# Halves of an attention head added by VectorE, one head split by GpSimd, a new order, and identity products among the first scores

## The chip, the cores and the metric

The kernel runs on one core of one Trainium2 chip. The metric is device time in microseconds (us) of one execution; the kernel before takes 1424.79 us, the median of 3 runs (1421.05 to 1426.22).

## The reference

Three blocks in a row, all in fp32:

```python
# attention: B=4, H=8, S=1152, D=64; 32 heads
q_pool = q.reshape(B, H, 576, 2, 64).mean(axis=3)
scores = q_pool @ k.T / 8;  attn = softmax(scores);  o = attn @ v        # 576 x 1152 per head
# mixer on x = (4, 576, 512)
h = relu(x.T @ w_tok1) @ w_tok2;  u = x + h.T;  x = u + relu(u @ w_ch1) @ w_ch2
# Fourier mixing, normalisation, channel block
u = x + real(fft2(x));  out = u + relu(norm(u) @ w1) @ w2
```

## The kernel before, in words

All fp32 products are made of fp32r parts: a number is split into a high part (ScalarE copies it with rounding) and a low part (the difference, by VectorE or GpSimd), and TensorE adds high·high, high·low and low·high.

`Plan` holds every operation of the program with an engine, a cost, a due time and the buffers that it takes. `order` issues, on each engine, the ready operation with the earliest due time; the table `SHIFT` adds a number to the due time of each kind of operation, so that table sets the order of the whole program. Each engine then works through its own list in order.

**The heads.** There are 32 heads (`g`), each with two units of 256 and 320 query columns (`UNITS`). The first eight (`g < ALONE`) run without a mixer beside them. For them `first_peaks` makes scores of 116 query rows by 384 keys (L684, 15 pairs of products a head), VectorE takes the maximum of each (L690), the maxima are turned by TensorE (L716) and laid into the query tile (L721), and `first_unit` makes the scores again, turned (L753), takes the exponential (L758) and multiplies by the values (L764). These values have a 65th column of ones, so the sum of each row comes out as a 65th row.

For the other 24 heads `peaks` makes the scores (L650) into one tile `m` of three banks, VectorE takes the maximum (L657), ScalarE the exponential and its sum (L660); `unit` turns it by TensorE (L803), ScalarE and VectorE split it (L807, L810), and the products with the values (L817) gather in one bank, `av`, of which there is one. The stationary side there holds the high parts of the values in columns 0 to 63 and the low parts in 64 to 127, so that the result has two halves, in partitions 0 to 63 and 64 to 127, that must still be added. ScalarE copies all 128 partitions into the tile `xtr` (L824).

**Turning the head.** `head_out` brings `xtr` back to rows of queries, in five blocks of 128 columns. For `g < ALONE` these are five transposes of 65 rows (L846). For the others they are five fp32 products with `twice`, two identities of 64 on top of each other (L848), which turn the tile and add its halves at once; an fp32 product stands in the trace as two. VectorE then scales the result (L860).

**The start.** `first_pair` loads the queries and keys of heads 0 and 1 and splits them for itself: sum of the two query halves (L560), high part (L562), low part (L564), and for the keys a high part (L572), a low part (L574) and a second copy (L576), the sums and the low parts on VectorE. Pairs of later heads are split by GpSimd (L600 to L610). `warm` puts 14 products of the identity, 512 columns each, in front of the scores (L586). Weights come as float64 and are made fp32 by ScalarE, GpSimd and VectorE all through the attention (L373 to L395).

Of the kernel before, what the change touches and what calls it, by code (L numbers as in the profile page):

```python
# [10 lines left out]
F32 = mybir.dt.float32  # L11
# [12 lines left out]
HQ = NQ // 2  # L24
# [20 lines left out]
ALONE = 8  # L45
NPH = 5
# [16 lines left out]
    "fourth": -81.45, "cvld": 14.04, "cabs": 225.41, "cclamp": 629.43, "cshift": 1065.51, "csign": 830.73,  # L63
    "cexp": 67.76, "cword": 44.09, "cmul": 212.45, "cadd": 527.83, "chi": 417.69, "csub": -302.75, "cvst":
    166.15, "cs": -293.69, "warm.": 694.45, "l.": -703.76, "q.": -145.41, "qh.": 219.14, "ql.": -134.29, "kh.":
    609.88, "kl.": -314.67, "M.": -448.03, "mr.": -385.51, "zh.": 237.47, "mr2.": -990.19, "zl.": -889.77,
    "mT.": 127.71, "mrow.": -636.35, "vld": -251.06, "S.": -1317.58, "exp.": 564.5, "AV.": 48.91, "xe.": 343.25,
# [7 lines left out]
    "sqrt": -1015.85, "fcld": -48.8, "fchi": -168.21, "fclo": 1157.76, "nyld": -154.7, "nyh": -411.21, "fld":  # L75
    152.94, "FPUT": 83.63, "DFT": -196.52, "Zh": 512.01, "Zl": -101.21, "PB": -31.29, "PA": -31.21, "bs": 8.24,
# [157 lines left out]
def tile_attention_moe_fnet(  # L234
# [43 lines left out]
    eps = base.tile([128, 1], F32, name="eps")  # L278
    rooted = base.tile([128, 1], F32, name="rooted")
    own = base.tile([128, len(QE)], F32, name="own")  # L280
    twice = base.tile([128, D], F32, name="twice")

# [1422 lines left out]
```

## Time and profile before

| | us |
|---|---|
| median of 3 runs (lowest, highest) | 1424.79 (1421.05, 1426.22) |
| the profiled execution, its own time | 1423.28 |
| its span in the trace | 1421.5 |
| TensorE matmuls busy in the span | 1388.5 |
| VectorE, ScalarE, GpSimd busy | 964.2, 770.1, 573.0 |

The span is what the trace covers; 1.8 us of the profiled execution's time lie around it. Busy times are unions, and a matmul's end is modelled, so that two matmuls one behind the other overlap in the trace.

### The profile page before, as it was taken

Reading aid. Unit: us, or ns where it says so; the run is one execution under the profiler, and the core shown is the slowest. Engines: PE = TensorE matmul, PEld = TensorE weight load, DVE = VectorE, ACT = ScalarE, POOL = GpSimd, SP = SyncE. Lnnn points to the kernel's source line nnn. Section 1 sums busy time; section 2 is a strip of 40 time slices with the busy share of each in tenths; the row PEclk is TensorE's granted clock in tenths of the full one; section 3 lists DMA queues with packets and bytes.
Section 4 is the critical chain, followed back from the end, with each engine's and each line's share of the span. In section 5 each row is a group of like instructions: output and inputs, shape, how many; then the busy total and the mean of one; then the engine's idle time right before and its main releaser. Section 6 shows DMA issues by size and latency. Waiting matters only on the chain.

```text
span 1421.5 us, 24599 instructions
## 1 busy us (share of the span) xinstructions
PE 1388.5 (98%) x9139; PEld 1284.5 (90%) x9139; DVE 964.2 (68%) x1782; ACT 770.1 (54%) x1534; POOL 573.0 (40%) x473
## 2 busy tenths in 40 slices
PE   7999999999999999999999999999999999999998
PEld 6777779999998999999999999999899888888887
DVE  7667568778886788777678884677757357656442
ACT  4554567666767667667666764322335245344330
POOL 4766776646765556677374561011110000000000
PEclk8999999999999999999999999999999999999999
DMA  6778777666678667776686545875274554543532
GB/s 184 209 200 223 196 221 232 205 188 211 205 204 249 191 191 215 207 215 207 197 239 192 160 149 171 259 234 158 78 237 124 208 183 167 196 156 137 204 115 93
DMA packets 112177, 270.36 MB, mean 190 GB/s; under 512 B 9971, under 2 KB 37748, under 8 KB 111767
## 3 DMA queue, kind: packets, MB, share of 16 engines
q1 hardware_dynamic: 112058, 268.79, 61.8%
q8 instruction: 72, 1.18, 0.3%
q14 instruction: 47, 0.39, 0.1%
HBM read 191.15 MB, written 44.86 MB: 166 GB/s over the span
## 4 chain that ended last, share of the span: by engine, by line
PE 87%; DMA 4%; DVE 3%; ACT 3%; issue 1%; SPq 1%; POOL 0%; ACTq 0%; DVEq 0%; POOLq 0%
PE bank L1449 9%; PE bank L1006 9%; PE m L650 8%; PE bank L986 8%; PE av L817 7%; PE y L1508 7%; PE bank L803 5%; PE c L1508 5%; PE av L764 3%; PE bank L684 2%; PE tr L986 2%; PE bank L1319 2%; PE y L1341 2%; PE s L753 2%; DMA slot<-in_wm_dram 2%; PE tr L803 2%
## 5 line engine op out<-in xcount | busy, mean ns | idle before, releaser
L657 DVE TENSOR_REDUCE nm<-m 128x1 f32<-128x1152 f32 (+1 forms) x120 | 162.3, 1352 | 36.6 <-PE m L650 33.5
L807 ACT ACTIVATE ph<-bank 128x320 fp32r<-128x320 f32 (+2 forms) x253 | 116.3, 477 | 100.7 <-PE bank L803 95.0
L660 ACT ACTIVATE s<-m,nm 128x1152 f32<-128x1152 f32 (+1 forms) x120 | 146.5, 1221 | 30.6 <-DVE nm L657 30.2
L1449 PE MATMUL bank<-tt,wc 128*128 128x320 f32 x1008 | 158.2, 311 | 4.6 <-DVE e L1463 4.6
L1449 PEld LDWEIGHTS bank<-tt,wc 128*128 128x128 f32 x1008 | 149.9, 188 | 12.8 <-DVE e L1463 10.6
L650 PE MATMUL m<-kk,qq 128*128 128x384 f32 (+1 forms) x720 | 151.0, 344 | 4.3 <-ACT s L660 4.2
L810 DVE TENSOR_TENSOR pl<-bank,ph 128x320 fp32r<-128x320 f32 (+2 forms) x253 | 130.7, 532 | 30.4 <-ACT ph L807 28.9
L1006 PE MATMUL bank<-h,w 128*128 128x256 f32 (+1 forms) x954 | 150.1, 300 | 0.0
L375 POOL TENSOR_SCALAR slot<-slot 128x512 f32<-128x512 f32 (+2 forms) x62 | 118.5, 1912 | 58.0 <-ACT slot L373 54.6
L986 PE MATMUL bank<-ut,w 128*128 128x256 f32 (+1 forms) x900 | 138.0, 297 | 0.0
L388 POOL TENSOR_TENSOR slot<-slot 128x512 f32<-128x512 f32 (+2 forms) x62 | 81.7, 1317 | 131.8 <-DVE slot L383 118.2
L1006 PEld LDWEIGHTS bank<-h,w 128*128 128x128 f32 x954 | 133.2, 189 | 0.3 <-DVE yt L1015 0.2
L817 PE MATMUL av<-ph,vv 128*128 128x256 f32 (+1 forms) x432 | 132.8, 324 | 0.0
L650 PEld LDWEIGHTS m<-kk,qq 128*128 128x128 f32 (+1 forms) x720 | 118.3, 179 | 11.3 <-ACT s L660 6.3
L986 PEld LDWEIGHTS bank<-ut,w 128*128 128x128 f32 x900 | 125.1, 189 | 0.0
L817 PE MATMUL av<-pl,vv 128*128 128x256 f32 (+1 forms) x432 | 120.2, 295 | 0.0
L803 PE MATMUL bank<-ident,s 128*128 128x128 f32 (+1 forms) x809 | 116.0, 262 | 2.6 <-DVE pl L810 2.4
L1463 DVE TENSOR_TENSOR e<-bank,e 128x320 f32<-128x320 f32 x96 | 47.2, 491 | 99.2 <-PE bank L1449 54.2
L1508 PE MATMUL y<-v,hp 128*128 128x512 f32 x432 | 104.2, 391 | 0.0
L803 PEld LDWEIGHTS bank<-ident,s 128*128 128x128 f32 (+1 forms) x809 | 96.7, 141 | 7.0 <-DVE pl L810 3.5
L1508 PEld LDWEIGHTS y<-v,hp 128*128 128x128 f32 x432 | 80.4, 188 | 16.4
L1015 DVE TENSOR_TENSOR yt<-bank,yt 128x320 f32<-128x320 f32 (+1 forms) x159 | 72.1, 455 | 28.7 <-PE bank L1006 26.7
(190 smaller groups left out, 2929.8 us busy)
## 6 DMA issues: line engine op xcount, KB each, us to landing
w<-wb_d SPq DMA_DIRECT2D x96, 512.0 KB, 4.9
slot<-in_wm_dram SPq DMA_DIRECT2D x56, 512.0 KB, 5.6
v<-w_d SPq DMA_DIRECT2D x24, 1024.0 KB, 5.5
raw<-w_d SPq DMA_DIRECT2D x24, 896.0 KB, 6.7
kk<-kx SPq DMA_DIRECT2D x66, 288.0 KB, 3.3
wb_d<-slot SPq DMA_DIRECT2D x24, 512.0 KB, 6.1
v<-in_v_dram SPq DMA_DIRECT2D x32, 292.5 KB, 3.9
qx<-in_qT_dram SPq DMA_DIRECT2D x15, 576.0 KB, 5.4
```

Source lines behind the costliest of these rows:

```text
L375: a = add("cclamp", "P", 0.155 + n * 0.00347, due, lambda: nc.gpsimd.tensor_scalar(out=f32(hi()), in0=f32(hi()), scalar1=F64_LO, scalar2=F ...
L650: nc.tensor.matmul(m.t[:n, :KW], qq.t[:r, t, q0:q0 + n], kk.t[:r, c * KW:(c + 1) * KW], start=(t == 0), stop=(t == 1))
L657: a = add("mx" + own_place, "V", t_dve(S), d + 0.05, lambda n=n, j=j: nc.vector.tensor_reduce(out=nm.t[:n, j:j + 1], in_=m_tile[0][:n, :, ...
L660: o = add("exp" + own_place, "A", t_act(S) + 0.18, d + 0.1, lambda s=s, n=n, j=j: nc.scalar.activation(out=s.t[:n].rearrange("p (c n) -> p ...
L803: nc.tensor.transpose(ps.t[:, at:at + r], made[j][0].t[:r, c * 128:(c + 1) * 128], ident[:r, :r])
L807: a = add("hi", "A", t_act(n), due + 0.1, lambda ps=ps, ph=ph, n=n: nc.scalar.activation(out=ph.t[:, :n], in_=ps.t[:, :n], func=AF.Copy), ...
L810: b = add("lo", "V", t_dve(n), due + 0.2, lambda ps=ps, ph=ph, pl=pl, n=n: nc.vector.tensor_tensor(out=pl.t[:, :n], in0=ps.t[:, :n], in1=f ...
L817: nc.tensor.matmul(po.t[:, :nq], vv.t[:, c].rearrange("p s d -> p (s d)"), x.t[:, k * nq:(k + 1) * nq], start=c == 0 and x is ph, stop=c = ...
L986: mms.append(lambda ps, k=len(mms), kk=kk, wi=wi, xi=xi, t0=t0, n=n: nc.tensor.matmul(ps[:, :n], view("p (s k n) -> p s k n", s=2, k=4)[:, ...
L1006: mms.append(lambda ps, k=len(mms), x=x, wi=wi, hi=hi, cc=cc, t0=t0, n=n: nc.tensor.matmul(ps[:, :n], ww[x][2]("p (s n) -> p s n", s=2)[:, ...
L1449: nc.tensor.matmul(ps.t[:, :PH], w.t[:, wi, k, 128 * kk:128 * kk + 128], x.t[:, xi, kk], start=(first and m == 0), stop=(last and m == 5), ...
L1508: nc.tensor.matmul(y.t, h.t[:, k, hi, j * 128:(j + 1) * 128], v.t[:, wi, k], start=(q == 0 and k == 0 and n == 0), stop=(q == 7 and k == 1 ...
```

## The change

It does five things.

- The 24 later heads are turned by five transposes of 65 rows, as the first eight are. `twice` is gone, and `xtr` has 65 partitions.
- So the halves are added before: ScalarE copies the upper 64 partitions of `av` (L836 of the changed file), and a new VectorE operation, `xa`, adds the lower 64 from `av` (L838), twice a head. `av` is held until that has run.
- Head 1's sum of query halves and the low parts of its keys (one operation of 576 columns, three of 384) go from VectorE to GpSimd.
- The warm-up has 22 products of 256 columns in place of 14 of 512, and 28 more such products stand among the score products of heads 0 and 1 (table `BETWEEN`).
- `SHIFT` has new numbers, so that every engine's list is in a new order.

```diff
+BETWEEN = ((0, 0, 0, 1, 0, 0, 13, 0, 0, 0, 0, 4, 1, 1, 0),
+           (8,) + (0,) * 14)
-    "fourth": -81.45, "cvld": 14.04, "cabs": 225.41, "cclamp": 629.43, "cshift": 1065.51, "csign": 830.73,
+    "fourth": -186.94, "cvld": 20.26, "cabs": 361.34, "cclamp": 955.96, "cshift": 1159.55, "csign": 719.06,
...
-            t = sp.tile([128, 640], F32, name=f"xtr{i}", bufs=1)
+            t = sp.tile([65, 640], F32, name=f"xtr{i}", bufs=1)
...
+                side = nc.gpsimd if g else nc.vector
...
-                    o = add("q.", "V", t_dve(b - a), d, lambda q=q: nc.vector.tensor_tensor(
+                    o = add(*(("q.", "V", t_dve(b - a)) if g == 0 else ("qp.", "P", t_pool(b - a))), d, lambda q=q, side=side: side.tensor_tensor(
...
-                    l = add("kl.", "V", t_dve(b - a), d, lambda k=k, kk=kk, a=a, b=b: nc.vector.tensor_tensor(
+                    l = add(*(("kl.", "V", t_dve(b - a)) if g == 0 else ("kp.", "P", t_pool(b - a))), d, lambda k=k, kk=kk, a=a, b=b, side=side: side.tensor_tensor(
...
-                for _ in range(WARM):
-                    nc.tensor.matmul(bank.t.rearrange("p (k n) -> p k n", k=4), ident_r,
-                                     ident_r[:, None, :].to_broadcast([128, 4, 128]), start=True, stop=True)
+                for _ in range(WARM * 8 // 5):
+                    idle_product()
...
+        spare = Buf(av_r)
+
+        def idle_product():
+            nc.tensor.matmul(spare.t[:, :256].rearrange("p (k n) -> p k n", k=2), ident_r,
+                             ident_r[:, None, :].to_broadcast([128, 2, 128]), start=True, stop=True)
...
+                    idle = BETWEEN[g][n_tops] if g < 2 else 0
+
-                    def scores(bank=bank, q0=QE[j], c=c):
+                    def scores(bank=bank, q0=QE[j], c=c, idle=idle):
+                        for _ in range(idle):
+                            idle_product()
...
-            return add("xe" + own_place, "A", t_act(nq), i + 1.7, lambda: nc.scalar.activation(
-                out=x.t[:, q0:q0 + nq], in_=po.t[:, :nq], func=AF.Copy), [o], new=[] if half else [x], uses=[po] + [x] * half)
+            def dst():
+                return x.t[:64, q0:q0 + nq]
+
+            a = add("xe" + own_place, "A", t_act(nq), i + 1.7, lambda: nc.scalar.activation(
+                out=dst(), in_=po.t[:64, :nq], func=AF.Copy), [o], new=[] if half else [x], uses=[po] + [x] * half)
+            return add("xa" + own_place, "V", t_dve(nq), i + 1.8, lambda: nc.vector.tensor_tensor(
+                out=dst(), in0=po.t[64:, :nq], in1=dst(), op=ALU.add), [a], uses=[po, x])
...
-                    if g < ALONE:
-                        nc.tensor.transpose(pt()[:, j, :], x.t[:65, cols], ident[:65, :65])
-                    else:
-                        nc.tensor.matmul(pt()[:, j, :D], x.t[:, cols], twice, start=True, stop=True)
+                    nc.tensor.transpose(pt()[:, j, :], x.t[:, j * 128:(j + 1) * 128], ident[:65, :65])
```

**The order, TensorE at the start.** `kk_148,qq_151` before and `kk_145,qq_148` in the change are head 0's keys and queries, `kk_149,qq_154` and `kk_146,qq_151` those of head 1; 116x384 are score products for the maxima, 128x288 those of the second scores. Before:

```order
L586 MATMUL bank<-ident_r 128x512 x14
L684 MATMUL bank<-kk_148,qq_151 116x384 x30
L684 MATMUL bank<-kk_149,qq_154 116x384 x4
L716 MATMUL bank<-ident_r,zc_144 74x116
L684 MATMUL bank<-kk_149,qq_154 116x384 x6
L753 MATMUL s<-qq_151,kk_148 128x288
```

In the change:

```order
L593 MATMUL av<-ident_r 128x256 x22
L693 MATMUL bank<-kk_145,qq_148 116x384 x6
L593 MATMUL av<-ident_r 128x256
L693 MATMUL bank<-kk_145,qq_148 116x384 x10
L593 MATMUL av<-ident_r 128x256 x13
L693 MATMUL bank<-kk_145,qq_148 116x384 x6
L593 MATMUL av<-ident_r 128x256 x8
L693 MATMUL bank<-kk_146,qq_151 116x384 x30
L593 MATMUL av<-ident_r 128x256 x4
L693 MATMUL bank<-kk_145,qq_148 116x384 x2
L593 MATMUL av<-ident_r 128x256
L693 MATMUL bank<-kk_145,qq_148 116x384 x2
L725 MATMUL bank<-ident_r,zc_141 74x116
L593 MATMUL av<-ident_r 128x256
L693 MATMUL bank<-kk_145,qq_148 116x384 x4
L762 MATMUL s<-qq_148,kk_145 128x288
```

Head 1's thirty products have moved ahead of head 0's last eight, and all sixty stand ahead of the first of the second scores, where forty stood before.

**The order, VectorE at the start.** `x_189` before and `x_194` in the change hold head 1's queries and keys; `mp<-bank` are the maxima. Before:

```order
L574 TENSOR_TENSOR kk_148<-x_166,kk_148 64x384
L574 TENSOR_TENSOR kk_149<-x_189,kk_149 64x384 x2
L690 TENSOR_REDUCE mp<-bank 116x1 x3
L574 TENSOR_TENSOR kk_149<-x_189,kk_149 64x384
L705 TENSOR_REDUCE bank<-mp 116x3
L560 TENSOR_TENSOR x_189<-x_189 128x576
L690 TENSOR_REDUCE mp<-bank 116x1 x2
L564 SCALAR_TENSOR_TENSOR qq_154<-x_189,qq_154 64x576
```

In the change:

```order
L575 TENSOR_TENSOR kk_145<-x_163,kk_145 64x384
L565 SCALAR_TENSOR_TENSOR qq_151<-x_194,qq_151 64x576
L699 TENSOR_REDUCE mp<-bank 116x1 x17
L714 TENSOR_REDUCE bank<-mp 116x3
L699 TENSOR_REDUCE mp<-bank 116x1
```

The four operations of head 1 that went to GpSimd are gone from here, and seventeen maxima stand in a row.

**The order, VectorE where an `xa` stands.** One place of 48, in the change:

```order
L383 TENSOR_SCALAR slot<-slot 128x512
L377 TENSOR_SCALAR slot<-slot 128x512
L819 TENSOR_TENSOR pl<-tr,ph 128x512
L838 TENSOR_TENSOR xtr_132<-av,xtr_132 64x320
L662 TENSOR_REDUCE nm<-m 66x1
```

The `xa` has its own place in VectorE's list, here between a low part and a maximum of the scores; the list before had no such row.

## Rows read from the trace of the kernel before

**Rows 1.** The page's part 1: busy time by engine.

```profile
PE 1388.5 (98%) x9139; PEld 1284.5 (90%) x9139; DVE 964.2 (68%) x1782; ACT 770.1 (54%) x1534; POOL 573.0 (40%) x473
```

**Rows 2.** Stages: length, busy PE, PEld, DVE, ACT, POOL (instructions); TensorE clock, DMA share, GB/s.

```profile
0.00:36.00 36.00, 28.81 (x110) 22.65 (x111) 26.94 (x62) 16.84 (x33) 16.08 (x22) 0.81 0.69 182
36.00:190.00 154.00, 145.98 (x786) 112.18 (x785) 97.20 (x188) 84.98 (x159) 114.46 (x87) 1.00 0.75 205
190.00:875.00 685.00, 678.29 (x5047) 661.25 (x5047) 526.55 (x916) 469.73 (x953) 414.69 (x328) 1.00 0.67 203
875.00:1421.00 546.00, 535.38 (x3201) 488.44 (x3200) 313.50 (x616) 198.51 (x392) 27.73 (x38) 1.00 0.52 171
```

**Rows 3.** The same columns for the start.

```profile
8.00:14.00 6.00, 3.82 (x17) 2.37 (x16) 5.40 (x11) 2.34 (x6) 0.00 (x0) 1.00 0.87 181
14.00:28.00 14.00, 11.60 (x36) 9.39 (x37) 11.36 (x25) 6.58 (x12) 8.55 (x5) 0.51 0.79 256
```

**Rows 4.** Stage 190 to 900, L848 alone: length, PE, PEld; clock, DMA share, GB/s.

```profile
190.00:900.00 710.00, 29.41 (x240) 29.08 (x240) 1.00 0.68 204
```

**Rows 5.** Timeline of TensorE, a later head's turn: start, duration, operation.

```profile
228.32 1.23 PE L848 MATMUL bank<-twice,xtr 128*128 128x64 f32 x10
229.38 0.61 PE L803 MATMUL bank<-ident,s 128*128 128x128 f32 x4
```

**Rows 6.** Timeline of TensorE, an early head's turn by transposes.

```profile
54.82 0.48 PE L846 MATMUL bank<-ident,xtr 65*128 65x65 f32 x5
55.13 1.62 PE L764 MATMUL av<-s,v 128*65 128x288 f32 x6
```

**Rows 7.** Groups of VectorE by shape: count, busy us, mean ns, idle before.

```profile
L1015 DVE TENSOR_TENSOR yt<-bank,yt 128x320 f32<-128x320 f32 x83 | 40.3, 486 | 13.0 <-PE bank L1006 12.0
L1015 DVE TENSOR_TENSOR yt<-bank,yt 128x256 f32<-128x256 f32 x76 | 31.8, 420 | 15.7 <-PE bank L1006 14.7
L657 DVE TENSOR_REDUCE nm<-m 128x1 f32<-128x1152 f32 x96 | 129.9, 1353 | 31.9 <-PE m L650 28.9 <-ACT vv L778 2.3
L574 DVE TENSOR_TENSOR kk<-x,kk 64x384 fp32r<-64x384 f32 x6 | 3.3, 556 | 1.0 <-ACT kk L572 0.8
```

**Rows 8.** ScalarE's copy of `av` (L824): durations min, median, max in ns.

```profile
L824 ACT ACTIVATE xtr<-av x48: 364/408/448, 203.5 to 863.1; 128x256 f32<-128x256 f32 x24, 128x320 f32<-128x320 f32 x24
```

**Rows 9.** Groups of TensorE by shape: values products and transposes of the scores.

```profile
L803 PE MATMUL bank<-ident,s 128*128 128x128 f32 x644 | 107.9, 273 | 2.6 <-DVE pl L810 2.4
L817 PE MATMUL av<-ph,vv 128*128 128x256 f32 x216 | 57.4, 295 | 0.0
```

**Rows 10.** Timeline of VectorE at the start.

```profile
7.15 0.82 DVE L564 SCALAR_TENSOR_TENSOR qq<-x,qq 64x348 fp32r<-64x348 f32 x2 [0.26 <-ACT qq L562]
...
9.68 3.81 DVE L690 TENSOR_REDUCE mp<-bank 116x1 f32<-116x384 f32 x8
...
17.92 0.76 DVE L560 TENSOR_TENSOR x<-x 128x576 f32<-128x576 f32 x1
...
19.53 1.77 DVE L564 SCALAR_TENSOR_TENSOR qq<-x,qq 64x576 fp32r<-64x576 f32 x1
...
24.14 0.52 DVE L721 TENSOR_TENSOR qq<-bank,own 10x348 fp32r<-10x348 f32 x1
```

**Rows 11.** Timeline of GpSimd at the start.

```profile
19.28 1.41 POOL L600 TENSOR_TENSOR qx<-qx 128x576 f32<-128x576 f32 x1 [15.16 <-DMA qx<-in_qT_dram]
...
22.91 2.64 POOL L610 TENSOR_TENSOR kx<-kx 128x1152 fp32r<-128x1152 f32 x1
```

**Rows 12.** Timeline of TensorE at the start.

```profile
10.38 2.37 PE L684 MATMUL bank<-kk,qq 128*116 128x384 f32 x10 [0.46 <-ACT kk L576]
...
16.69 1.63 PE L684 MATMUL bank<-kk,qq 128*116 128x384 f32 x4 [0.30 <-DVE mp L690]
...
25.59 2.12 PE L753 MATMUL s<-qq,kk 128*128 128x288 f32 x8
...
29.78 1.22 PE L684 MATMUL bank<-kk,qq 128*116 128x384 f32 x6
```

More of the change, by code (lines that the diff above doesn't have):

```diff
@@ L280, in tile_attention_moe_fnet @@
     own = base.tile([128, len(QE)], F32, name="own")
-    twice = base.tile([128, D], F32, name="twice")
     with tc.manual_schedule():
@@ L290, in tile_attention_moe_fnet @@
         nc.vector.memset(eps, 1e-6)
-        nc.gpsimd.tensor_copy(out=twice[:D], in_=ident[:D, :D])
-        nc.gpsimd.tensor_copy(out=twice[D:], in_=ident[D:, D:])
         nc.vector.tensor_reduce(
@@ L581, in warm @@
         def warm():
[L582 removed]
             def products():
[L585 to L589 removed]
+                for _ in range(WARM * 8 // 5):
+                    idle_product()
+            add("warm.", "T", 4.5, -50, products, new=[spare])
+        spare = Buf(av_r)
+        def idle_product():
+            nc.tensor.matmul(spare.t[:, :256].rearrange("p (k n) -> p k n", k=2), ident_r,
+                             ident_r[:, None, :].to_broadcast([128, 2, 128]), start=True, stop=True)
         def pair(p):
@@ L688, in first_peaks @@
                     o = add("M" + own_place, "T", t_pe(2, KW), dd, scores, q_op + k_ops[c] + [z], held if len(tops) > 1 else [],
-                            new=[bank], uses=[kk, qq])
+                            new=[bank], uses=[kk, qq] + [spare] * (idle > 0))
                     tops.append(add("mr" + own_place, "V", t_dve(KW), dd, lambda bank=bank, j=j, c=c: nc.vector.tensor_reduce(
@@ L764, in av @@
                         nc.tensor.matmul(po.t[:65, :HQ], w.t[:, c0 + j], ex()[:, j], start=c0 + j == 0, stop=c0 + j == NK - 1)
-                o = add(f"AV{own_place}{gr}", "T", t_pe(3.7 * n, HQ), due + 0.8, av, [a] + v_ops, [o],
+                o = add(f"AV{own_place}{gr}", "T", t_pe(3.62 * n, HQ), due + 0.8, av, [a] + v_ops, [o],
                         new=[] if gr else [po], uses=[w, s] + [po] * bool(gr))
             return add("xe" + own_place, "A", t_act(HQ), i + 1.7, lambda: nc.scalar.activation(
-                out=x.t[:65, qs], in_=po.t[:65, :HQ], func=AF.Copy), [o], new=[] if half else [x], uses=[po] + [x] * half)
+                out=x.t[:, qs], in_=po.t[:65, :HQ], func=AF.Copy), [o], new=[] if half else [x], uses=[po] + [x] * half)
         def values(g):
@@ L843, in turned @@
                 for j in range(5):
-                    cols = slice(j * 128, j * 128 + 128)
-                    if g < ALONE:
-                        nc.tensor.transpose(pt()[:, j, :], x.t[:65, cols], ident[:65, :65])
-                    else:
-                        nc.tensor.matmul(pt()[:, j, :D], x.t[:, cols], twice, start=True, stop=True)
+                    nc.tensor.transpose(pt()[:, j, :], x.t[:, j * 128:(j + 1) * 128], ident[:65, :65])
             first = h == 0
-            turn = o = add("turn", "T", 0.3 if g < ALONE else 0.6, due, turned, evacs, prev, new=[bank] + xx * first, uses=[x])
+            turn = o = add("turn", "T", 0.42, due, turned, evacs, prev, new=[bank] + xx * first, uses=[x])
             if g < ALONE:
```

25 lines of the change are left out of this document (12 added, 13 removed), and 14 rows, old and new, of the table SHIFT.

## The prediction

> **What bounds the kernel now.** I read the busy times first: TensorE is busy for 1388.5 us, VectorE for 964.2, the other two for less [rows 1]. An average can hide stages, so the table by stage comes next [rows 2]. From 190 to 875 us, where the 24 later heads run beside the mixer, TensorE is busy for 678.3 of 685.0 us at a granted clock of 1.00, VectorE for 526.6 (77%), ScalarE and GpSimd for less. What is taken from TensorE there shortens the run, unless something else comes up behind it. It sits idle for 6.7 us in that stage, for 8.0 from 36 to 190, for 10.6 from 875 on, and for 7.2 in the first 36 us. That start is the one place with another limit: from 14 to 28 us the granted clock is 0.51, the lower of its two levels (1.2 of 2.4 GHz), after 6 us in which TensorE was busy for only 3.82; VectorE is busy for 5.40 of those 6 us and for 11.36 of the next 14 [rows 3]. So VectorE, with the maxima and the splits of two heads, sets the pace at the start, and TensorE everywhere else.
>
> **The turn of the later heads: minus 17.9 us.** L848 has 240 records in 24 heads and 29.4 us of TensorE, 1.23 a head [rows 4, 5]; from its start to that of the next operation it is 1.06 us. The five transposes that replace it stand in the early heads at 0.48 us, 0.31 from start to start [rows 6], with the same tile shape, 65 rows by 128 columns, as the change uses. By busy time that saves 24 x (1.23 - 0.48) = 18.0 us, or 17.9 from the 29.41 of the stage's row; by starts 24 x 0.75 = 18.0. I take 17.9; all of it lies in the stage in which TensorE is never free for long.
>
> The new operations are transposes, and it matters whether they hold the clock. The stage has some 650 transposes of 128 by 128 in one group alone (107.9 us of TensorE) [rows 9], and its granted clock is 1.00 throughout [rows 2]. The Trainium skill (TensorE: Matmul & The Clock Gate, Part 4) says the opposite: that the full clock does not engage for transposes, since they do not count as work in the same way. By that rule the stage before could not have kept its clock; this trace disagrees, and I go by the trace. What such a drop would cost is a rival below.
>
> **The halves: plus 1 us.** Nowhere in the trace is there an `xa`; the nearest rows are VectorE's adds of a bank and a tile, 486 ns for 320 columns and 420 for 256 [rows 7]. It comes to 24 x 0.906 = 21.7 us of VectorE in the stage, which goes from 526.6 of 685 us to 548.3 of 667, or 82%. VectorE has the room; the question is the wait. There is one `av` bank, and the next unit's first product with the values has to wait until ScalarE's copy (0.41 us [rows 8]) and now also `xa` are through. Behind the waiting `xa` stand VectorE's maxima and low parts, and for these TensorE waits in turn. Lower bound nothing: the copy on the same bank kept no product waiting (idle 0.0 before L817 [rows 9]), because other products stand in between. Upper bound 21.7 us, if every `xa` lay bare. I take 1 us, near the lower end: the nearest row is the copy, on the same bank and of about the same length, and it was covered in all 48 units. The copy itself costs ScalarE the same, as its length is set by columns.
>
> **The start: minus 1 us.** VectorE loses 0.76 us (the sum of 576 columns [rows 10]) and 3 x 0.556 = 1.67 us (low parts of the keys [rows 7]), 2.4 in all. GpSimd takes them: 1.41 us for 576 columns, 2.64 for 1152 [rows 11], so some 1.0 for 384, 4.4 us in all, and it did nothing between 4 and 19 us (its 15.16 us of idle time in the row). Its next work is the split of the second pair, which moves back; so does the load of that pair's keys, in SP's list now behind three loads of weights. That pair is needed only after head 1's second scores have begun, and I cost it at nothing; without that cover it is up to 5 us.
>
> What the new order wins or loses is counted at one point. Head 0's second scores began at 25.59 us [rows 12] with 40 of the 60 products for the maxima issued. Now all 60 go first, and the maxima pace them: 30 of them at 0.476 us from 9.68 on [rows 10] are 14.3 us, with 0.56 for a low part, 0.82 for the low part of head 1's queries, some 1.5 for small operations and 0.52 for laying the maxima in, 27.4 in all. So the second scores begin 1.8 us later, but 20 products, about 3.7 us at the full clock (1.22 for six [rows 12]), are behind TensorE, and the eight second scores that had run by then cost 1.3 of it. That leaves about 0.6, and I take 1. Upper bound: the 2.4 us and 0.95 more, 3.4, where that low part is not held up; lower bound minus 3, if TensorE runs at the lower level again and paces the maxima (1.63 us for four products [rows 12] is 0.41 each, 0.82 a maximum against 0.476).
>
> The 0.82 us needs a word. 348 and 228 columns together took 0.82 us, but 576 at once took 1.77, and it began while GpSimd's sum ran from 19.28 to 20.69 [rows 10, 11]; what is left after 20.69 is 0.61. The Trainium skill (SBUF — State Buffer, Who interferes with whom) has the rule: a VectorE operation with two SBUF inputs and a GpSimd operation that reads SBUF lock each other out. The row agrees. It speaks against this change: by it, head 1's low parts on GpSimd hold up that operation by up to 1.0 us again, and the gain at the start would be gone.
>
> **Idle products: nothing.** The 28 products of the identity stand where TensorE waits: from 8 to 28 us it is idle for 4.6 us of its 20 [rows 3]. If they stood in the way they would cost up to 28 x 0.2 = 5.6 us at the lower level, by half of a 384-column product there (0.41). The warm-up gets shorter, and the scores behind it wait for the split keys, not for it. `twice` and its two copies were off the path.
>
> **The new order elsewhere: nothing.** It can win at most the idle 25.3 us outside the start and lose as much; the counts of all other operations are the same. I put it at 5 us either way.
>
> **The sum.** -17.9 + 1 - 1 = -17.9 us. The profiled execution took 1423.3 us, so 1405.4; that execution is 1.5 us below the median of the runs shown, against which it is 1406.9. I say 1406.
>
> **Rivals.**
>
> *The turn's time comes back only in part.* TensorE is faster, and VectorE at 82% comes up behind it: a score tile's maximum takes 1.35 us [rows 7], its three banks are free only after the exponential, and an `xa` in front of the maximum makes that longer. For: VectorE already sits idle for 31.9 us before those maxima because of TensorE and now gets less of that. Against: 18% of its time stays free. Half of the turn lost is 1415; all but a quarter, 1420. Chance 0.17, of which 0.10 less than 0.5% faster.
>
> *Slower: `av` becomes the bound.* Each of 48 units waits before its first product with the values for copy and `xa`, and `xa` stands in VectorE's list behind whatever is late there. From 0.38 us a unit (18.0 / 48) the gain is gone; if an `xa` of 0.45 us and a third of a maximum lie bare, 0.9 us, it is 43 us against 18 won, 1450. Against: no product waited for the copy. Chance 0.10, 0.03 of it near no change.
>
> *The start goes wrong.* The sixty products hold head 0 back, or the second pair is late: plus 5, 1411. Chance 0.05.
>
> *The clock falls at the turns.* At the start a drop lasted 14 us at half speed; one at each of 24 turns would take 24 x 7 = 168 us, 1574. The rule above on transposes would have it so. Against: the clock of 1.00 over all of the transposes there. Chance 0.01.
>
> **How the numbers follow.** The forecast has 0.67, and its own range is 1397 to 1414: the start between +3 and -3.4, the order 5 us either way. 0.5%, about what a measurement of this kernel tells from no change, is 7 us, so no change is 1418 to 1432. Faster is 0.67 + 0.07 + 0.05 = 0.79; within 0.10 + 0.03 = 0.13; slower 0.07 + 0.01 = 0.08. The range from 1395 to 1418 takes in the better bound of start and order together and most of the partial case; about 0.2 is left outside.
>
> **What would show it.** Right: the 24 turns at about 0.48 us, 11.5 in all; no wait before the products with the values; the stage from 190 us some 17 us shorter with VectorE near 82%; clock 1.00 between 14 and 28 us. Wrong: idle time before the products with the values put down to the `xa` line, or before the maxima and transposes by more than 5 us; turns above 0.8 us; TensorE below 97% in that stage; a granted clock under 1.00 after the first 30 us.

## The result, and the profile after

| | before | after |
|---|---|---|
| median (lowest, highest), us | 1424.79 (1421.05, 1426.22) | 1411.56 (1411.43, 1415.37) |
| the profiled execution, us | 1423.28 | 1411.55 |
| its span, us | 1421.5 | 1409.2 |

The ratio after to before is 0.9917, 95% interval [0.9898, 0.9937]: faster by 13.2 us by the medians and 9 to 14.5 by the interval, where 18.8 were forecast. The sign was right, and the time lies inside the range (1395 to 1418); the gain is about two thirds of what was worked out.

Page, part 1, of the changed kernel (it answers to [rows 1]):

```profile
PE 1375.2 (98%) x9055; PEld 1270.4 (90%) x9055; DVE 975.8 (69%) x1826; ACT 766.7 (54%) x1534; POOL 576.6 (41%) x475
```

The stages of the changed kernel, with the columns of [rows 2], and the start, with those of [rows 3]:

```profile
0.00:36.00 36.00, 31.60 (x160) 25.86 (x161) 31.29 (x69) 17.57 (x34) 22.81 (x26) 0.95 0.68 182
36.00:190.00 154.00, 145.69 (x776) 112.42 (x775) 89.49 (x176) 84.36 (x156) 110.85 (x86) 0.98 0.75 208
190.00:875.00 685.00, 674.63 (x4993) 653.66 (x4992) 549.14 (x973) 474.60 (x967) 413.93 (x328) 1.00 0.69 206
```

The turns are what they were said to be. L858 alone over 710 us, as [rows 4], and one turn, as [rows 5]:

```profile
190.00:900.00 710.00, 11.58 (x120) 10.64 (x120) 1.00 0.70 208
...
234.79 0.47 PE L858 MATMUL tr<-ident,xtr 65*128 65x65 f32 x5
235.10 0.61 PE L812 MATMUL bank<-ident,s 128*128 128x128 f32 x4
```

29.41 us have become 11.58, so TensorE was relieved of 17.8 us, against a forecast of 17.9; the clock is 1.00 over the stage. VectorE took on 549.14 - 526.55 = 22.6 us there, against 21.7 forecast. But TensorE's idle time in the same 685 us went from 6.7 to 10.4 us. So the price was right and the relief did not all become time. Three points of the program place it: the first score product of a later head, and the first product of the last channel block (y<-w,h), which follows the heads and the mixer. First and last starts stand behind the durations. Before:

```profile
L650 PE MATMUL m<-kk,qq x720: 331/339/553, 180.1 to 845.5; 128*128 128x384 f32 x144, 128*66 128x384 f32 x36
...
L1341 PE MATMUL y<-w,h x144: 387/393/482, 1014.6 to 1110.4; 128*128 128x512 f32 x144
```

After:

```profile
L655 PE MATMUL m<-kk,qq x720: 332/339/583, 178.8 to 836.7; 128*128 128x384 f32 x144, 128*66 128x384 f32 x36
...
L1351 PE MATMUL y<-w,h x144: 387/393/481, 1001.7 to 1098.2; 128*128 128x512 f32 x144
```

Ahead of the first point 1.3 us were won in this pair of profiles, where 1 was forecast. Between the two, 834.5 us became 822.9: 11.6 us won out of 17.8. Behind the second, 406.9 and 407.5 us are left of the spans, no gain or loss to speak of. The missing 6 us lie in the stage of the later heads, below called **the stage**.

What TensorE waits for there, from 190 to 875 us (engine, line, releaser; us in total, times, longest). Before, this is the whole list of 0.2 us and more:

```profile
PE bank L803 <- DVE pl L810: 2.4, 3, 1.2
PE m L650 <- ACT s L660: 2.4, 5, 0.9
PE tr L1006 <- DVE yt L1015: 1.0, 1, 1.0
PE tr L803 <- DVE pl L810: 0.6, 1, 0.6
```

After, the seven longest:

```profile
PE m L655 <- ACT s L665: 2.2, 4, 1.1
PE av L826 <- DVE pl L819: 1.8, 3, 0.7
PE bank L931 <- ACT x L873: 1.1, 1, 1.1
PE bank L959 <- DVE pl L819: 0.9, 1, 0.9
PE bank L858 <- DVE xtr L838: 0.9, 1, 0.9
PE tr L812 <- DVE pl L819: 0.6, 2, 0.3
PE bank L931 <- POOL x L875: 0.4, 1, 0.4
```

No product with the values (L826) waits for an `xa` (L838); one turn does, at the very end. What is new is that products with the values wait for VectorE's low parts (L819), and that the hand-over to the third sequence's channel step (L931) waits for ScalarE and GpSimd.

### The profile page after: what moved, and what is told of

The parts are those of the page before. It is cut to its first block, busy times and chain, and to the rows that moved or that the text cites. A ratio compares the mean times of both kernels' runs of the same rounds, so it can differ in the third digit from the quotient of the medians.

```text
span 1409.2 us, 24476 instructions
## 1 busy us (share of the span) xinstructions
PE 1375.2 (98%) x9055; PEld 1270.4 (90%) x9055; DVE 975.8 (69%) x1826; ACT 766.7 (54%) x1534; POOL 576.6 (41%) x475
## 4 chain that ended last, share of the span: by engine, by line
PE 89%; DVE 4%; ACT 3%; DMA 2%; issue 1%; POOL 1%; SPq 0%; ACTq 0%; POOLq 0%; DVEq 0%
PE bank L1459 10%; PE bank L1016 9%; PE m L655 9%; PE bank L996 8%; PE av L826 8%; PE y L1518 7%; PE bank L812 5%; PE c L1518 5%; PE av L773 4%; PE bank L693 3%; PE bank L1329 2%; PE y L1351 2%; PE tr L1016 2%; PE tr L996 2%; PE s L762 2%; PE c L1172 2%
## 5 line engine op out<-in xcount | busy, mean ns | idle before, releaser
L819 DVE TENSOR_TENSOR pl<-bank,ph 128x320 fp32r<-128x320 f32 (+2 forms) x256 | 132.9, 536 | 20.1 <-ACT ph L816 19.1
L1016 PE MATMUL bank<-h,w 128*128 128x256 f32 (+1 forms) x906 | 144.7, 300 | 0.0
L826 PE MATMUL av<-ph,vv 128*128 128x256 f32 (+1 forms) x432 | 132.5, 324 | 0.2 <-ACT ph L816 0.2
L1016 PEld LDWEIGHTS bank<-h,w 128*128 128x128 f32 x906 | 126.9, 189 | 0.2 <-DMA w<-wb_d 0.2
L826 PE MATMUL av<-pl,vv 128*128 128x256 f32 (+1 forms) x432 | 120.5, 296 | 2.0 <-DVE pl L819 1.8
L1469 ACT ACTIVATE e<-bank 128x320 f32<-128x320 f32 x72 | 31.3, 434 | 109.4 <-PE bank L1459 109.4
```

The source lines that it names most:

```text
L819: b = add("lo", "V", t_dve(n), due + 0.2, lambda ps=ps, ph=ph, pl=pl, n=n: nc.vector.tensor_tensor(out=pl.t[:, :n], in0=ps.t[:, :n], in1=f ...
L826: nc.tensor.matmul(po.t[:, :nq], vv.t[:, c].rearrange("p s d -> p (s d)"), x.t[:, k * nq:(k + 1) * nq], start=c == 0 and x is ph, stop=c = ...
L1016: mms.append(lambda ps, k=len(mms), x=x, wi=wi, hi=hi, cc=cc, t0=t0, n=n: nc.tensor.matmul(ps[:, :n], ww[x][2]("p (s n) -> p s n", s=2)[:, ...
```

## The experiments

Ratios are to the kernel before on the same chip, with 95% intervals. The questions: is the missing 6 us the price of the `xa`? What does the turn bring by itself? Do the other parts of the order pay? What is the start worth?

**1. The add cut to one column.** Same order; 255 or 319 columns of each half are not added.

```diff
-                out=dst(), in0=po.t[64:, :nq], in1=dst(), op=ALU.add), [a], uses=[po, x])
+                out=dst()[:, :1], in0=po.t[64:, :1], in1=dst()[:, :1], op=ALU.add), [a], uses=[po, x])
```

> The changed kernel with one edit: the VectorE addition of the halves (48 times, 256 or 320 columns) is made on one column only, in the same place of the same order. The addition of the other columns is left out. Theory A (the addition and the waits behind it eat the 6 us that are missing between the 18 us that the transposes should save and the 12 us that the stage from 186 us on got shorter): 1404 to 1408 us, 4 to 7 below the changed kernel's 1411.6, and TensorE's waits before the transposes of the scores and inside the turns are mostly gone. Rival B (the new order lost those 6 us elsewhere, the addition is hidden): 1411 to 1412, no change.

Measured: 1410.78 us (1408.12 to 1413.4), 0.9902 [0.9886, 0.9917]. An operation on one column still takes 160 ns, so 7.7 of the 22.0 us that `xa` has on VectorE are left, and so is its wait for ScalarE. With the other 14 us gone, the time is 0.8 us from the changed kernel's, well inside the intervals. The length of the `xa` is not the missing 6 us; experiment 2 has an equally short operation in the same place, read by nothing, and takes the kernel before's time.

**2. The changed order with the old turn.** The one-column operation stands in the place of `xa`, and its result is used nowhere, so only the turn differs from experiment 1.

```diff
+    twice = base.tile([128, D], F32, name="twice")
-                    nc.tensor.transpose(pt()[:, j, :], x.t[:, j * 128:(j + 1) * 128], ident[:65, :65])
+                    if g < ALONE:
+                        nc.tensor.transpose(pt()[:, j, :], x.t[:65, j * 128:(j + 1) * 128], ident[:65, :65])
+                    else:
+                        nc.tensor.matmul(pt()[:, j, :D], x.t[:, j * 128:(j + 1) * 128], twice, start=True, stop=True)
```

> The changed kernel, in its own order, with the old turn: ScalarE copies all 128 partitions, TensorE turns and adds the halves by products with the two identities, and in place of VectorE's addition stands an operation on one column into a scratch tile. Nothing of the result is left out. Both theories: 18 us above the run with the one-column addition, since that difference is the turn alone on TensorE. Theory A: so 1422 to 1426. Rival B: 1428 to 1430.

Measured: 1424.26 us (1420.55 to 1427.49), 0.9992 [0.998, 1.0004]. This is the key run, in two ways. The new order and the new start with the old turn are worth nothing: the kernel before again. And the turn, with everything else held, is worth 1424.26 - 1410.78 = 13.5 us by medians and 1419.6 - 1407.9 = 11.7 by the spans of the two profiles, not 18. The two ratios differ by 0.0090, give or take 0.0020, which is 12.8 us, give or take 2.8: that it is less than 17.8 is clear of the noise, by how much is not. All theories had taken 18 here, and all were wrong. The stage is 835.4 us here and 823.2 in experiment 1; from start to start the turns take 29.3 and 11.5 us in it, so 17.8 us less of them made it 12.2 shorter, and the other products stand 5.6 us further apart: transposes of the scores by 1.7, products with the values by 1.4, the mixer's first products and the scores by 1.3 each. ("From start to start" is the time from a product's start to that of the next one.)

TensorE's lists in these two runs are the same but for the turns, so their traces can be laid beside each other product by product. Each of the first 23 turns brings its 0.75 us. Of the 5.6 us, 1.6 are lost at the first scores of the stage and 1.2 at the hand-over: at both places the granted clock is at the lower level in experiment 1 (0.5 from 187.0 to 190.4 us and from 859.4 to 862.9) and 1.00 in experiment 2. Some 2.8 are waits, at six places, the last turn among them, which lies over a wait and brings 0.3. The changed kernel itself has the first of the two stretches; its clock from 188 to 192 us is 0.57 (columns of [rows 2]):

```profile
188.00:192.00 4.00, 4.00 (x16) 3.85 (x17) 2.64 (x3) 2.78 (x6) 3.62 (x4) 0.57 0.58 164
...
187.94 2.18 PE L655 MATMUL m<-kk,qq 128*128 128x384 f32 x6 [1.48 <-ACT s L665]
...
191.48 2.76 PE L931 MATMUL bank<-x,w 128*128 128x512 f32 x11
```

Experiment 2 at the same place, with the clock at 1.00:

```profile
186.04 1.35 PE L659 MATMUL m<-kk,qq 128*128 128x384 f32 x6 [1.48 <-ACT s L669]
...
188.02 2.75 PE L938 MATMUL bank<-x,w 128*128 128x512 f32 x11
```

Behind the same wait of 1.48 us, the same products take 3.54 us in the one and 1.98 in the other. The first turn of a later head comes at 234.79 us in the changed kernel, so this loss is not the price of the turn. Of the nine profiles with the changed kernel's lists (or with one change in them) and the new turn, eight have such a stretch between 185 and 198 us and experiment 3 has none; what decides it stays open. The division of the 5.6 us is read from one profile of each run.

The waits of this kernel in the same 685 us:

```profile
PE m L659 <- ACT s L669: 1.9, 4, 1.1
PE av L830 <- DVE pl L823: 1.1, 2, 0.6
PE bank L938 <- ACT x L880: 1.1, 1, 1.1
PE bank L966 <- DVE pl L823: 0.9, 1, 0.9
PE av L830 <- ACT ph L820: 0.7, 1, 0.7
PE bank L938 <- POOL x L882: 0.4, 1, 0.4
```

The waits at the hand-over (1.1 and 0.4) are here too, so they belong to the new order. What the faster turn adds to the rows of waits is a little more of several of them, for low parts above all.

**3. Each turn made three times over.** The same rate from the other side: later heads transpose each block three times into the same place.

```diff
-                for j in range(5):
+                for j in [j for j in range(5) for _ in range(1 if g < ALONE else 3)]:
```

> The changed kernel with each of the five transposes of the 24 later turns made three times into the same place: 240 more transposes at 62 ns, 14.9 us more of TensorE, nothing else. Theory I (TensorE sets the pace there and every microsecond counts): 1426 to 1427. Rival K (about a third of what is taken from or given to TensorE there is made up by its waits, as the 13.5 for 17.8 us between the two earlier runs say): 1420 to 1423.

Measured: 1421.0 us (1418.06 to 1425.0), 0.9981 [0.9969, 0.9992]: 9.4 us more than the changed kernel, for 14.6 us more of TensorE from start to start. In its profile the stage is 834.7 us, 11.8 more, and the start happened to be shorter. So 14.6 us put on TensorE cost 0.65 of themselves by medians and 0.8 in the stage (0.6 against the repeat in experiment 12, whose stage is 825.9 us); 17.8 taken off it gave 0.66 to 0.76. TensorE's time is not passed on in full in either direction.

**4. The new turn in the old order's table.** The kernel before with the turn by transposes and `xa`; the old `SHIFT`, old start.

> The kernel before with the turn alone changed: transposes of 65 rows, the addition of the halves on VectorE, the cost of the turn in the plan 0.42; the old table, the old start. Theory G (TensorE's shorter turn pays in any order of this kind): 1410 to 1415 us, 11 to 15 below the kernel before. Rival H (the table of due times must fit the work; with the old numbers the new operations fall badly): within 5 us of before or slower, 1420 to 1435.

Measured: 1433.48 us (1430.76 to 1436.63), 1.0062 [1.005, 1.0074]: slower than before by 8.9 us, though its turns are as short as the changed kernel's. A new operation and new costs give another list on every engine, and this one has VectorE 548.65 us busy and TensorE 669.85 in the 685, with these waits on top:

```profile
PE m L647 <- ACT s L657: 5.0, 5, 2.2
PE av L814 <- DVE pl L807: 2.9, 6, 0.7
```

**5. The new table alone.** The kernel before with the new `SHIFT`; nothing else changed.

> The kernel before with the new table of due times alone: the old turn, the old start, no additions. Theory G (the order is worth little by itself): 1420 to 1428. Rival H (the table must fit the work): slower than before by over 7 us, 1432 or more.

Measured: 1461.28 us (1452.66 to 1464.21), 1.0247 [1.0225, 1.0269], 36.7 us slower. The same row of waits has grown from 2.4 us before to 10.0:

```profile
PE m L651 <- ACT s L661: 10.0, 8, 2.9
```

Two parts that cost 8.9 and 36.7 us, each alone, gain 13 together (with the new start). Experiment 2 shows why that is no riddle: there the changed kernel's very list is kept, and with the old turn in it that list costs nothing. A table makes a list only together with the operations and costs it was made for; with others it makes a different list.

**6. Head 1's split on VectorE again, under its old names.**

```diff
-                side = nc.gpsimd if g else nc.vector
+                side = nc.vector
...
-                    l = add(*(("kl.", "V", t_dve(b - a)) if g == 0 else ("kp.", "P", t_pool(b - a))), d, lambda k=k, kk=kk, a=a, b=b, side=side: side.tensor_tensor(
+                    l = add("kl.", "V", t_dve(b - a), d, lambda k=k, kk=kk, a=a, b=b, side=side: side.tensor_tensor(
```

> The changed kernel with head 1's sum and low parts of the keys back on VectorE, with the due times that this kind of operation has in the changed table. Theory E (VectorE paces the start): the second scores begin 2.4 to 3.4 us later than 27.3 us, time 1413.5 to 1415. Rival F (GpSimd's share holds VectorE up as long as it relieves it): 1411 to 1412.

Measured: 1433.93 us (1425.8 to 1436.89), 1.0058 [1.0042, 1.0075]. It tells nothing of the split: with the names the due times changed and with them every list, and the stage, which has no part of head 1, is 845.0 us. Its second scores even began earlier, at 25.96 us. So the split was tried again with the lists held.

**7. Head 1's split on VectorE, in the same places.** Only the engine of the four operations changes.

```diff
-                side = nc.gpsimd if g else nc.vector
+                side = nc.vector
```

> The changed kernel with head 1's sum and low parts on VectorE again, each at its own place in the order of all operations, so that all other lists stay as they are. Theory E (VectorE paces the start, and it is relieved of 2.4 us): second scores at 29 to 30 us instead of 27.3, time 1413 to 1414.5. Rival F (what VectorE is relieved of it loses to GpSimd's reads, 1.7 us in the two operations that took 1.43 and 1.45 us): second scores at 27.3 to 28.3, time 1411 to 1412.5.

Measured: 1414.97 us (1411.39 to 1417.8), 0.9931 [0.9916, 0.9946]. The six runs spread too far to tell the time from the changed kernel's. The second scores begin at 28.11 us, 0.8 later than in the changed kernel's first profile. Most of that is not the split: they begin at 27.99 us in the repeat of the changed kernel (experiment 12) and at 27.93 in experiment 1, which has the same start. The granted clock from 8 to 14 us was 0.62 here, 0.66 and 0.63 in those two, and 0.72 in the first profile. At a like clock the split is worth 0.1 to 0.2 us. What became of the 2.4 us taken off VectorE shows in the rows. VectorE in the changed kernel:

```profile
9.01 0.56 DVE L575 TENSOR_TENSOR kk<-x,kk 64x384 fp32r<-64x384 f32 x1 [0.46 <-ACT kk L573]
...
14.21 1.43 DVE L575 TENSOR_TENSOR kk<-x,kk 64x384 fp32r<-64x384 f32 x1
15.67 1.45 DVE L565 SCALAR_TENSOR_TENSOR qq<-x,qq 64x576 fp32r<-64x576 f32 x1
...
28.86 2.46 DVE L377 TENSOR_SCALAR slot<-slot 128x512 int32<-128x512 int32 x1
```

and GpSimd beside it:

```profile
14.20 3.79 POOL L575 TENSOR_TENSOR kk<-x,kk 64x384 fp32r<-64x384 f32 x3 [1.71 <-ACT kk L573]
...
28.38 2.65 POOL L615 TENSOR_TENSOR kx<-kx 128x1152 fp32r<-128x1152 f32 x1
```

The same low part takes 0.56 us alone and 1.43 beside GpSimd's; with the split on VectorE, L565 takes 0.75 us in place of 1.45. GpSimd pays too: 1.26 us for each 384 columns, where 1.0 was estimated. Of the 2.4 us, (1.43 - 0.56) + (1.45 - 0.75) = 1.6 went back to VectorE; that the other 0.8 reached the second scores is not shown.

**8. No products of the identity among the scores.**

```diff
-                    idle = BETWEEN[g][n_tops] if g < 2 else 0
+                    idle = 0
```

> The changed kernel without the 28 products of the identity among the first scores (the 22 ahead of them stay). Theory C (they hold the clock): the granted clock falls to 0.5 for some 14 us between 10 and 28 us, TensorE paces the maxima of head 1 at 0.8 us instead of 0.48, the second scores begin after 30 us instead of at 27.3, and the time is 3 to 6 us longer, 1415 to 1418. Rival D (VectorE paces the start anyway): 1411 to 1413.

Measured: 1413.62 us (1413.4 to 1415.97), 0.9925 [0.9911, 0.9939]. The granted clock is 0.58 from 8 to 14 us and 0.69 from 14 to 28 (0.72 and 1.00 in the changed kernel's first profile, 0.66 and 0.90 in its repeat; 1.00 and 0.51 before [rows 3]). So it falls much as the first theory said, but the second scores begin at 28.22 us, not after 30, against 27.30 and 27.99 in the two profiles of the changed kernel. The time rises by about 2 us, which the intervals don't separate from nothing; the median lies below the theory's 1415 to 1418 us, but a loss of 3 us is not excluded.

**9. Eight more products in the warm-up.**

```diff
-                for _ in range(WARM * 8 // 5):
+                for _ in range(WARM * 8 // 5 + 8):
```

> The changed kernel with 30 in place of 22 products of the identity ahead of the first scores: about 1 us more of TensorE between 7.4 and 8.6 us, where it waits 1.2 us for the split keys. Theory M (the granted clock falls at about 10 us because TensorE stood idle before it, and this costs the start some microseconds: the runs of the changed kernel and of its variants reach the first scores of the later heads anywhere from 174 to 184 us): no stretch at the lower level before 28 us, second scores begin at or before 27 us, and the run is 1 to 4 us faster than the changed kernel. Rival (the low stretch at 10 us lies under VectorE's maxima, which pace TensorE there, and the low stretches later on, at 137 and 188 us, are what moves the start): the start's clock may change, the second scores begin at 27.3 us within 0.3, the time is that of the changed kernel within 1.5 us.

Measured: 1413.7 us (1409.22 to 1415.75), 0.9908 [0.9891, 0.9925]. The clock and the second scores did what theory M said, the time did not. And the same start came about elsewhere without the eight products. The first scores of the changed kernel, below them those of this one, and then those of experiment 3, which has the changed kernel's start (columns of [rows 3]):

```profile
8.00:14.00 6.00, 5.14 (x20) 4.71 (x21) 5.18 (x10) 3.13 (x8) 1.40 (x1) 0.72 1.02 254
```

```profile
8.00:14.00 6.00, 5.01 (x30) 4.07 (x30) 5.39 (x12) 3.03 (x7) 1.41 (x1) 1.00 1.01 248
```

```profile
8.00:14.00 6.00, 5.15 (x30) 4.23 (x30) 5.09 (x11) 2.89 (x7) 1.42 (x1) 1.00 0.99 249
```

TensorE stood idle for 1.2 us before 8.6 us in the changed kernel, and its clock was 0.72 in the next 6; here it was idle for 0.7, the clock stayed at 1.00, and the second scores began at 25.95 us, 1.35 earlier. In experiments 2, 3 and 11, with 22 products as in the changed kernel, TensorE was idle for 0.8 to 1.0 us, the clock was 1.00 as well, and the second scores began at 25.57, 25.79 and 25.70 us. So the effect of the eight products is not told from what one execution or another does by itself. The lead was still 1.2 us ahead of the load at 170 us (168.52 us for 169.75, the last four scores before it). But the first scores of the later heads came at 180.7 us, not 178.8: the lead was lost, and more, in the last 12 us. ScalarE in the changed kernel, and below it in this one:

```profile
170.31 0.68 ACT L386 ACTIVATE slot<-slot 128x512 f32<-128x512 uint32 x1 [0.68 <-DMA slot<-in_wm_dram]
```

```profile
170.54 0.65 ACT L386 ACTIVATE slot<-slot 128x512 f32<-128x512 uint32 x1 [2.13 <-DMA slot<-in_wm_dram]
```

A load of weights lands within 0.3 us of the same time in both, so who comes earlier waits longer. TensorE, which needs the exponential behind it, waits 1.63 us there, 0.18 in the changed kernel, and twelve products with the values behind it then take 4.76 us, 3.08 in the changed kernel; the granted clock from 174 to 177 us is 0.50 here and 1.00 there.

**10. The exponential ahead of the weights.** Such a place stands at 131 us too, with a longer wait. ScalarE in the changed kernel:

```profile
134.46 0.66 ACT L386 ACTIVATE slot<-slot 128x512 f32<-128x512 uint32 x1 [2.46 <-DMA slot<-in_wm_dram]
...
135.58 0.63 ACT L767 ACTIVATE s<-s 128x576 f32<-128x576 f32 x1
```

ScalarE stands 2.46 us before a load of weights; an exponential that is ready stands two places behind it, and TensorE waits 2.67 us for that. So one swap, on ScalarE's list alone (the list, not the code):

```diff
-ACTIVATE slot<-slot 128x512 x2
 ACTIVATE s<-s 128x576
+ACTIVATE slot<-slot 128x512 x2
```

> The changed kernel with one swap on ScalarE's list: at 131 to 136 us of the changed kernel ScalarE stands 2.5 us in front of a piece of weights that has not landed (L386), with an exponential of early scores (L767, 576 columns) two places behind it, for which TensorE waits 2.7 us; here that exponential stands ahead of the two weight operations. Theory N (what the start wins is given back at this load, so the gain of the start ends in a wait for a transfer): TensorE's wait there falls from 2.7 us to under 0.8, the first scores of the later heads come 2 us earlier, and the run is 1 to 2.5 us faster than the changed kernel's 1411.5 to 1412. Rival (the wait moves on: the weights' GpSimd steps come later, and the next load or the next exponential behind them holds TensorE as long): the 2.7 us is gone at this place, the first scores of the later heads come within 1 us of where they came, and the time is 1410.5 to 1414.

Measured: 1411.83 us (1409.63 to 1413.54), 0.9912 [0.9895, 0.9928]. The wait is down as theory N said, and another has come up 2 us behind it, as the rival said:

```profile
134.92 0.81 PE L779 MATMUL s<-qq,kk 128*128 128x288 f32 x4 [0.80 <-ACT s L784]
...
136.90 1.19 PE L790 MATMUL av<-s,v 128*65 128x288 f32 x4 [1.11 <-ACT xtr L794]
```

In this one profile the later heads begin at 177.0 us, 1.8 earlier than in the changed kernel's, but experiment 1, without the swap, has 177.7; in the median nothing of it is seen. Whether it is worth a microsecond stays open.

**11. The hand-over.** In the changed kernel TensorE waits at the end of the last head:

```profile
859.87 0.40 PE L858 MATMUL bank<-ident,xtr 65*128 65x65 f32 x3 [0.93 <-DVE xtr L838]
861.35 0.50 PE L931 MATMUL bank<-x,w 128*128 128x512 f32 x1 [1.09 <-ACT x L873]
862.30 3.92 PE L931 MATMUL bank<-x,w 128*128 128x512 f32 x16 [0.44 <-POOL x L875]
```

Here the last five steps of four transposes each of the mixer's result (L1050) are issued behind the last head's last products with the values, to lie over the first of these waits; the other engines' lists keep their order. TensorE's list (not the code):

```diff
+MATMUL av<-ph,vv 128x320
+MATMUL av<-pl,vv 128x320
 MATMUL tr<-ident,yt 96x128 x4
...
 MATMUL tr<-ident,yt 96x128 x4
-MATMUL av<-ph,vv 128x320
-MATMUL av<-pl,vv 128x320
 MATMUL bank<-ident,xtr 128x65 x5
```

> The changed kernel with one move on TensorE's list: the five late transposes of the last mixer's result and what hangs on them stand behind the last head's last product with the values, in place of ahead of it. Theory L (part of the missing gain was given back at the hand-over from the last head to the third sequence's channel step: TensorE waits 0.9 us for an xa, 1.1 for ScalarE's x and 0.4 for GpSimd's x between 858 and 863 us of the changed kernel, because the mixer's work that lay over them before had been used up): those waits fall from 2.5 us to about 1, and the run is 1 to 2 us faster than the changed kernel, 1409 to 1411 us. Rival (TensorE's idle time only moves, as elsewhere in this kernel): the waits fall and others of the same size stand behind them, in the channel step; 1411 to 1415 us.

Measured: 1412.64 us (1409.04 to 1415.69), 0.9911 [0.9893, 0.993]. The same place:

```profile
855.22 0.40 PE L875 MATMUL bank<-ident,xtr 65*128 65x65 f32 x3 [0.27 <-DVE xtr L855]
856.70 0.50 PE L948 MATMUL bank<-x,w 128*128 128x512 f32 x1 [1.08 <-ACT x L890]
858.23 7.97 PE L948 MATMUL bank<-x,w 128*128 128x512 f32 x21 [1.02 <-POOL x L892]
```

The wait for `xa` fell from 0.93 to 0.27 us, and the one for GpSimd's `x` rose from 0.44 to 1.02: 2.4 us in sum, as before. The rival holds at this place: by these rows the chain from the last `av` to the split `x` sets it. The mixer's products behind it took longer as well, at a granted clock of 0.50 from 858 to 862 us, where the changed kernel's profile has 1.00 behind its wait.

**12. The changed kernel once more.**

> The changed kernel itself, unaltered, once more: the floor of the comparisons on this chip. If the differences of 1 to 3 us among its variants are differences of the granted clock between executions, this repeat differs from the first measurement (1411.43 to 1415.37 us) by as much, with stretches at the lower level in other places; if they belong to the variants, it repeats 1411 to 1412 with the low stretches at 10.6, 137 and 188 us.

Measured: 1411.93 us (1410.18 to 1413.53), 0.9903 [0.9887, 0.9918]. Its profiled execution took 1413.45 us, with a clock of 0.66 from 8 to 14 us and 0.90 from 14 to 28, where the first had 0.72 and 1.00. So the same program differs between executions by 2 to 5 us, and by its clock. With the profiles of experiments 1, 2, 3 and 11 there are six of the same start (in experiment 2 with two short copies on GpSimd more): their second scores begin between 25.57 and 27.99 us, early where the clock is 1.00 from 8 to 14 us and late where it is 0.63 to 0.72, and their later heads between 174.3 and 178.8 us. The stage differs too: it is 822.9 us in the first profile of the changed kernel and 825.9 in the second, which has more of it at the lower clock. Differences of 1 to 2 us between variants above are within this; those of 9 us and more are not. No variant is faster than the changed kernel by more than its scatter.

## Why the prediction was right, and where it was off

**What bounds the kernel: right, with a limit.** TensorE is the longest engine in the stage, and time taken off it shortens the run. But "98% busy" is not "passes all its time on": 17.8 us off brought 11.7 to 13.5, 14.6 us on cost 9 to 12.

**The turn: the step that failed.** Its price on TensorE was right to 0.1 us. The step was that "all of it lies in the stage in which TensorE is never free for long", by which the 17.9 was taken in full. Experiments 1 and 2 give 13.5 by medians for it, 12.2 in the stage of one pair of profiles. This is the first rival in a milder form, about a quarter lost where half was its case. Its mechanism was only partly right: the waits before the maxima, which it named, did not grow (2.4 us before, 2.2 after); those for low parts and several smaller ones did, some 2.8 of the 5.6 us in that pair. The other 2.8 are two stretches at the lower granted clock, for which the prediction had no term, and the first of them (1.6 us) lies ahead of the first changed turn. How the loss divides in other executions is not known.

**The transposes and the clock: right of the turns, not of the rest.** The clock of the stage still rounds to 1.00 with the transposes of the turn added to those of the scores, and no drop came with each turn. But the prediction named a clock under 1.00 after the first 30 us as a sign of being wrong, and it is there: 0.98 from 36 to 190 us, where [rows 2] have 1.00, at the lower level once behind the wait of 2.67 us at 136 us and once at 188. Both lie ahead of the first changed turn, so those transposes are not the cause. The Trainium skill (TensorE: Matmul & The Clock Gate, Part 4) says that the full clock does not engage for transposes. This trace does not bear that out, but it does not test it alone: the transposes of the scores and of the turns are some 1200 of 4993 instructions here, with other products between them. That the stage "could not have kept its clock" by the rule was more than the rule says.

**The halves, plus 1: not contradicted.** In numbers of partitions, ScalarE copies 0 to 63 of `av` and `xa` adds 64 to 127. An `xa` takes 426 ns for 256 columns and 494 for 320, against 420 and 486 taken from the nearest rows:

```profile
L838 DVE TENSOR_TENSOR xtr<-av,xtr 64x320 f32<-64x320 f32 x24 | 11.8, 494 | 3.3 <-ACT xtr L836 2.6
L838 DVE TENSOR_TENSOR xtr<-av,xtr 64x256 f32<-64x256 f32 x24 | 10.2, 426 | 6.6 <-ACT xtr L836 6.0
```

It waits 8.6 us for ScalarE in sum, and TensorE waits for it once, 0.9 us. Cutting it to one column brought 0.8 us, not told from nothing. The slower rival, `av` as the bound, had no footing: 0.2 us before L826 are put down to ScalarE's high parts, 1.8 to the low parts, none to `xtr`.

**The start, minus 1: near, in part by luck.** The second scores began at 27.30 us, worked out as 27.4; but the same start gave 25.57 to 27.99 us in other executions, with the granted clock, which stood in the prediction's lower bound alone. The later heads came 1.3 us earlier than in the one profile of before, and up to 5.8 earlier in others of the same start. The lock that the prediction weighed came as told and larger: 1.6 us of VectorE, where up to 1.0 was feared. The rule of the Trainium skill (SBUF — State Buffer, Who interferes with whom) held for the pair of operations with two inputs; the section also names tensor-scalar operations, with one tensor input, among those that can contend, and the row L377 agrees: 2.46 us beside GpSimd's 1152 columns, where the median of its kind is 0.43. That the split itself won anything is not shown (experiment 7). It was not said that what the start wins must still pass the loads at 131 and 170 us; in experiment 9 the wait at the second was longer by 1.45 us, more than the lead that was left.

**The idle products, nothing: near enough.** Without them the clock was lower in the one profile taken, and the time some 2 us longer, within the scatter. Their worst price was put too low: 256 of 384 columns are two thirds of a product, not half, so that 28 of them at the lower level are 7.6 us by the prediction's own 0.41, not 5.6.

**The new order elsewhere, nothing: right as a term, wrong as a part.** With the list kept and the old turn in it, it is worth 0.9992 [0.998, 1.0004], the new start included. But as a table it cannot be taken alone (plus 36.7), nor can the turn without it (plus 8.9). The 5 us either way would have been far too narrow for a list that was not made for its operations.

## What to carry to other kernels

Time taken off an engine that is 98 to 99% busy is worth less than itself when the others run at 70 to 80% beside it, with waits for each other in both directions: here about three quarters by the medians, and about two thirds for time put on, so one run that doubles or triples the operation gives an idea of the rate before the change is written. When a program's order comes from a table, compare parts with every engine's list held and only the operation exchanged; a part tried under the wrong table measures the table. A gain at the start counts only at the first point behind which nothing waits for a transfer. And before a microsecond at the start is put down to a change, several profiles of one and the same start should lie beside each other: here they differ by more than the variants do.

## What was not expected of the hardware

- The granted clock is not the same from one execution of a program to the next: 0.72 and 1.00 in two stretches of the start in one, 0.66 and 0.90 in the other. Behind the same wait of 1.48 us, the same products ran at the lower level in one kernel's profile and at 1.00 in another's (187.94 and 186.04 us, experiment 2). A stage whose mean rounds to 1.00 can hide such a stretch. In the profiles of the kernels with these lists, or with one swap in them, the later heads began between 174.3 and 184.2 us. The nine runs of the changed kernel lie between 1410.18 and 1415.37 us.
- A VectorE operation beside GpSimd took 2.5 to 6 times as long (1.43 us for 0.56, 2.46 for 0.43), and GpSimd pays as well (1.26 us for an estimated 1.0): of 2.4 us moved from the one to the other inside the start, 1.6 came back, and the second scores at a like clock moved by 0.1 to 0.2.
